# Seven products instead of eight in nearly every second expert product of a Sinkhorn-attention and mixture kernel, with the first product running a little ahead

## The chip, the core and the metric

The kernel runs on one core of a Trainium2 chip. The metric is the device time of one execution in microseconds (us). Engines are named as in the profile: PE (TensorE matmuls), PEld (TensorE weight loads), DVE (VectorE), ACT (ScalarE), POOL (GpSimd), SP (SyncE, which only issues transfers here).

## The reference, cut to what matters

```python
def _attn_ref(q, k, v, sort_net):            # 4 batches, 8 heads, 768 rows, 64 columns
    P = sort_net                             # 8x8 per head
    for _ in range(5):
        ...                                  # exp, then rows and columns divided by their sums
    k_sorted, v_sorted = ...                 # blocks of 96 rows mixed by P
    ...                                      # softmax attention inside each block
def _moe_ref(x, w_gate, w1, w2):             # x: 3072x512; w1: 8x512x1024; w2: 8x1024x512
    P = np.exp(x @ w_gate - max)
    for _ in range(8):
        ...                                  # P balanced over rows and columns
    for e in range(8):
        h = np.maximum(x @ w1[e], 0.0)
        out += P[:, e:e + 1] * (h @ w2[e])
```

Attention makes x; a balanced gate makes P; then each of eight experts does two matrix products with a relu between them, and its result is added to the output, weighted per row.

## The kernel before, in words

The first part does the attention and, woven into it, expert 0. It ends at about 134 us of the span. The stretch from there to about 173 us finishes expert 0, balances the gate (`balance`, eight rounds of short DVE operations with a small matmul in each) and starts expert 1. The rest, to the end, is experts 1 to 7.

For those experts a *product* is one pair (e, p): expert e on 1024 of the 3072 rows, so there are 21. Both matrix products of a pair can be done as a 2x2 block product by seven smaller products instead of eight, with sums of blocks made beforehand (Winograd's form of Strassen's scheme). The names of that scheme are s1 to s4 for sums of the left blocks, t1 to t4 (or x1 to x4) for sums of the right blocks, and u, v, w, x for accumulators in PSUM.

- `hidden(e, p, i, hT)` is a quarter of the first product with the relu. It is a generator of seven steps, here h0 to h6, each with two matmuls of 512 columns (L482). ACT copies three accumulators out (p1 L502, u2 L510, p5 L515), DVE makes c11, c22 and c12 from PSUM and a copy (L506, L518, L521: an addition with a floor at 0), and ACT makes c21 from the last accumulator u by a relu (L524). The four blocks go to the tile hT, which has two buffers.
- `output(e, p, i, hT)` is a quarter of the second product in the plain way: two results of 128 rows, eight matmuls of 512 columns each (L542), and for each one `gather`.
- `output7(e, p, i, hT)` is the same quarter by seven products: seven steps, here k0 to k6, each with four matmuls of 256 columns (L573). It has two accumulators, u (256 columns) and x (512 columns). u is taken out by DVE and goes on accumulating, so each later step on u waits for the gather before it. There are five gathers of 256 columns and one of 512. The pool of accumulators `oacc` has three buffers, so the x of a quarter gets the buffer that the u of the quarter before gives back.
- `gather` (L529) is one DVE operation: osbl += gate * PSUM.
- `sum_h(i, hT)` (L559) makes s1 to s4 for one quarter on POOL, four operations of 128x512. `sum_w` and `sum_w2` make the sums of the weights on POOL, eight operations each for an expert; they are taken one at a time from a queue by `sums(n)`.
- `scale0` (L602) multiplies expert 0's output by its gate on ACT; `sum_x` (L434) makes the sums of x on DVE.

In the loop `for n in range(1, 3 * (E - 1))` the quarter i of product n (`hidden`) is interleaved, step by step, with the quarter i of the second product of the pair before. The second product uses `output` for i = 0, for the whole of the first pair and for the whole of the last pair, and `output7` for the rest: 27 quarters in the plain way, 57 by seven products. After the loop the last pair's second product runs alone, in the plain way.

The order of each engine's queue is made by a scheduler when the program is built, from the order in which the code issues the operations; operations marked `pin` keep their order. Each engine works through its own queue in that order. A scheduler's rule seen in the built queues is that two engines do not read the same PSUM tile at once: the second waits for the first.

Of the kernel before, what the change touches and what calls it, by code (L numbers as in the profile page):

```python
# [25 lines left out]
def kernel(  # L26
# [55 lines left out]
    def load_w1(e):  # L82
        w1t[e] = wp.tile([128, 4, F], BF16, name="w1e")
        pin(nc.gpsimd.dma_start(out=w1t[e],
                                in_=moe_w1[e].rearrange("(kk k) f -> k kk f", k=128)))
# [37 lines left out]
        nc.vector.reciprocal(out=cs, in_=cs)  # L123
        nc.vector.tensor_mul(Pt, Pt, mkap(cs, [cs.ap[0], cs.ap[1], [0, 8]]))

    Prep = pp.tile([32, 8, 8, 16], BF16)
    for eng, i0 in ((nc.vector.tensor_copy, 0), (nc.scalar.copy, 4)):
        eng(Prep[:, i0:i0 + 4], mkap(P, [P.ap[0], [8, 4], [1, 8], [0, 16]], off=i0 * 8))

    xtT = xtp.tile([128, 4, N], BF16)  # L130
    osbl = xtp.tile([128, NT, Dm], F32)
    glog = xtp.tile([128, NT, E], F32)
    Pb = pp.tile([128, 32, 8], F32)
    Rt = {}

    def build_r(bb, eng, n):
# [230 lines left out]
    with ExitStack() as c2:  # L367
# [4 lines left out]
        for bb in range(1, B):  # L372
# [22 lines left out]
            for _ in ex:  # L395
# [5 lines left out]
        tc.tile_pool(name=name, bufs=bufs, reuse_waits="tile"))  # L401
    mpc, xcp, wq, wcq = late("mpc", 1), late("xcp", 1), late("wq", 2), late("wcq", 1)
    htp, fsp, hsp, w2q = late("htp", 2), late("fsp", 1), late("hsp", 3), late("w2q", 1)
    bk = ctx.enter_context(tc.tile_pool(name="bk", bufs=5, space=bass.MemoryType.PSUM,
                                        reuse_waits="tile"))
    op = ctx.enter_context(tc.tile_pool(name="op", bufs=3, space=bass.MemoryType.PSUM,
# [8 lines left out]
    def sum_w2(e):  # L415
        w2s[e] = (wcp.tile([128, 4, 4, Dm // 2], BF16, name="w2e") if e % 2 else
                  w2q.tile([128, 4, 4, Dm // 2], BF16, name="w2s"))
        for k in (0, 2):
            b11, b12 = (w2t[e][:, k:k + 2, d:d + 256] for d in (0, 256))
            b21, b22 = (w2t[e][:, 4 + k:6 + k, d:d + 256] for d in (0, 256))  # L420
            t1, t2, t3, t4 = (w2s[e][:, j, k:k + 2, :] for j in range(4))
            for a, b, c in ((b12, b11, t1), (b22, t1, t2), (b22, b12, t3), (b21, t2, t4)):
                pin(nc.gpsimd.tensor_tensor(out=c, in0=a, in1=b, op=ALU.subtract))
                yield
# [46 lines left out]
            yield  # L471

    TOP = 3.0e38

    def hidden(e, p, i, hT):
        ta, tb = (slice(1024 * p + 512 * j, 1024 * p + 512 * j + 512) for j in range(2))
        fs = slice(128 * i, 128 * i + 128)
        xs = slice(512 * p, 512 * p + 512)

        def add(ps, wa, xa, first):  # L480
            for kk in range(2):
                nc.tensor.matmul(ps, wa[:, kk, :], xa[:, kk, :],  # L482
                                 start=(first and kk == 0), stop=(kk == 1),
                                 skip_group_check=True)

        def wide(name):
            return fsp.tile([128, 512], F32, name=name)

        w1 = w1t[e]
        s1, s2, s4 = (wct[e][:, j, :, fs] for j in range(3))  # L490
        x1, x2, x4 = (xc[:, j, :, xs] for j in range(3))
        s3, x3 = w1[:, 0:2, 512 + 128 * i:640 + 128 * i], xtT[:, 0:2, tb]
        a11, a12 = w1[:, 0:2, fs], w1[:, 2:4, fs]
        a22 = w1[:, 2:4, 512 + 128 * i:640 + 128 * i]
        b11, b21, b22 = xtT[:, 0:2, ta], xtT[:, 2:4, ta], xtT[:, 2:4, tb]
        c11, c12 = hT[:, i, 0:512], hT[:, i, 512:1024]
# [12 lines left out]
        u2 = wide("u2")  # L509
        nc.scalar.copy(u2, u)  # L510
        yield
        v = bank()
        add(v, s1, x1, True)
        p5 = wide("p5")
        nc.scalar.copy(p5, v)  # L515
        yield
        add(u, s3, x3, False)
        nc.vector._custom_dve(TENSOR_ADD_SAT, out=c22, in0=u, in1=p5, s0=TOP, s1=0.0)  # L518
        yield
        add(v, s4, b22, False)  # L520
        nc.vector._custom_dve(TENSOR_ADD_SAT, out=c12, in0=v, in1=u2, s0=TOP, s1=0.0)  # L521
        yield
        add(u, a22, x4, False)
        nc.scalar.activation(out=c21, in_=u, func=AF.Relu)  # L524
        yield

    def gather(e, t, c, ps):
# [20 lines left out]
            yield  # L548


    hs = {}

    def sum_h(i, hT):
        s = hs[i] = hsp.tile([128, 4, 4, 128], BF16, name="hs")
        a11, a21, a12, a22 = (hT[:, f:f + 4, t + 128 * i:t + 128 * i + 128]
                              for f in (0, 4) for t in (0, 512))
        for a, b, o, c in ((a21, a22, ALU.add, 0), (s[:, 0], a11, ALU.subtract, 1),
                           (a11, a21, ALU.subtract, 2), (a12, s[:, 1], ALU.subtract, 3)):
            nc.gpsimd.tensor_tensor(out=s[:, c], in0=a, in1=b, op=o)  # L559

    def output7(e, p, i, hT):
        a, b = 8 * p + i, 8 * p + 4 + i
        ha, hb = slice(128 * i, 128 * i + 128), slice(512 + 128 * i, 640 + 128 * i)
        s1, s2, s3, s4 = (hs[i][:, j] for j in range(4))
        t1, t2, t3, t4 = (w2s[e][:, j] for j in range(4))
        u = op.tile([128, Dm], F32, name="oacc")[:, 0:256]
        x = op.tile([128, Dm], F32, name="oacc")
        x0, x1 = x[:, 0:256], x[:, 256:512]
        b11, b21, b22 = w2t[e][:, 0:4, 0:256], w2t[e][:, 4:8, 0:256], w2t[e][:, 4:8, 256:512]

        def add(ps, h, w, first):
            for fb in range(4):
                nc.tensor.matmul(ps, h[:, fb, :], w[:, fb, :], start=(first and fb == 0),  # L573
                                 stop=(fb == 3), skip_group_check=True)

        add(u, hT[:, 0:4, ha], b11, True)
        gather(e, a, 0, u)
        yield

        add(x0, hT[:, 4:8, ha], b21, True)  # L580
        yield
        add(u, s2, t2, False)
        gather(e, a, 256, u)
        yield
        add(x1, s1, t1, False)
        gather(e, b, 256, x1)
        yield
        add(u, s3, t3, False)
        gather(e, b, 256, u)
        yield  # L590
        add(x1, s4, b22, False)
        gather(e, a, 0, x)
        store(e, a)
        yield
        add(u, hT[:, 4:8, hb], t4, False)
        gather(e, b, 0, u)
        store(e, b)
        yield

    def scale0(ts):  # L600
        for t in ts:
            nc.scalar.activation(out=osbl[:, t, :], in_=osbl[:, t, :], func=AF.Copy,  # L602
                                 scale=glog[:, t, 0:1])

    def take(works):
        while works:
            works = [w for w in works if next(w, 0) is None]
# [18 lines left out]
            next(xs, 0)  # L626
    take([chain, xs])
    xs = sum_x(2)
    last = (1, 0, hT)
    queue = [sum_w2(1)]  # L630

    def sums(n):
        while n and queue:
            if next(queue[0], 0) is None:
                n -= 1
            else:
                queue.pop(0)

    for n in range(1, 3 * (E - 1)):
        e, p = 1 + n // 3, n % 3  # L640
        if n == 1 or p == 0 and e + 1 < E:
            load_w1(e + 1)
            queue.append(sum_w(e + 1))
        hT = htp.tile([128, 8, 1024], BF16, name="hT")
        for i in range(4):
            if last[0] == 1:
                scale0([8 * last[1] + i, 8 * last[1] + 4 + i])
            if n > 1 and i < 3:
                sum_h(i + 1, last[2])
            next(xs, 0)  # L650
            sums(3 if n == 1 or i == 3 else 1)
            take([hidden(e, p, i, hT),
                  (output7 if n > 1 and i else output)(*last[0:2], i, last[2])])
        if n == 1 or p == 0 and e + 1 < E:
            load_w2(e + 1)
            queue.append(sum_w2(e + 1))
        last = (e, p, hT)
    for i in range(4):
        take([output(*last[0:2], i, last[2])])


# [28 lines left out]
```

## Time and profile before

| | |
|---|---|
| time, median of 3 runs | 690.42 us (690.34 to 690.60) |
| the profiled execution's own time | 690.48 us |
| its span | 688.7 us |
| granted TensorE clock | 0.993 |
| PE busy | 666.7 us (97%) |
| DVE busy | 474.5 us (69%) |
| POOL busy | 432.4 us (63%) |
| ACT busy | 298.0 us (43%) |

The span runs from the first to the last instruction. The profiled execution took 1.8 us more than its span, and that lies around the span. Matmuls are pipelined, so "PE busy" says that PE had work in flight and not how fast it went; the time from the start of one matmul to the start of the next says that.

### The profile page before, as it was taken

How to read it: one execution, taken by the hardware profiler on the slowest of the kernel's cores; microseconds unless marked ns; L12 is line 12 of the kernel's file. 1: busy time of each engine (PE TensorE's matmuls, PEld its weight loads, DVE VectorE, ACT ScalarE, POOL GpSimd, SP SyncE). 2: the span in 40 equal slices, each digit the busy share in tenths (PEclk: the TensorE clock that was granted, in tenths of full speed). 3: DMA queues.
4: the chain of work that ended last, by engine and by line, in shares of the span. 5: the costliest groups of instructions: out<-in, count | busy, mean ns of one | idle time of the engine just before them, and what ended most of it. 6: DMA issues, size and time to landing. Idle time of an engine off the chain costs nothing.

```text
span 688.7 us, 12265 instructions
## 1 busy us (share of the span) xinstructions
PE 666.7 (97%) x4784; PEld 404.4 (59%) x4784; DVE 474.5 (69%) x968; ACT 298.0 (43%) x550; POOL 432.4 (63%) x411
## 2 busy tenths in 40 slices
PE   2999999999999999999999999999999999999997
PEld 1757666644446556556656655655665665565563
DVE  6627555578757778667767776767776777676773
ACT  3747646345953333343333433333333433334330
POOL 4532324202737987978977987789795998637520
PEclk9899999999999999999999999999999999999999
DMA  9897833403210340030302140034003120001213
GB/s 146 164 218 120 140 77 63 62 1 62 30 32 1 62 61 1 1 63 9 54 0 35 28 62 1 1 62 61 1 1 62 25 38 0 1 1 63 91 65 151
DMA packets 31755, 36.51 MB, mean 53 GB/s; under 512 B 2000, under 2 KB 24016, under 8 KB 31696
## 3 DMA queue, kind: packets, MB, share of 16 engines
q0 software_dynamic: 26400, 27.82, 25.5%
q1 hardware_dynamic: 5296, 7.90, 3.4%
q8 instruction: 37, 0.61, 0.4%
q14 instruction: 22, 0.18, 0.1%
HBM read 52.45 MB, written 6.29 MB: 85 GB/s over the span
## 4 chain that ended last, share of the span: by engine, by line
PE 91%; DVE 5%; ACT 1%; DMA 1%; issue 1%; SPq 0%; DVEq 0%
PE bk L482 36%; PE oacc L573 25%; PE oacc L542 13%; PE bank L297 5%; PE bank L304 5%; PE bank L232 2%; PE bank L152 1%; PE bank L243 1%; PE bank L215 1%; PE bank L196 1%; DMA vsb<-vs 1%; DVE cs L464 0%; PE bk L297 0%; PE bk L466 0%; PE bank L183 0%
## 5 line engine op out<-in xcount | busy, mean ns | idle before, releaser
L529 DVE SCALAR_TENSOR_TENSOR osbl<-oacc,glog,osbl 128x256 f32<-128x256 f32 (+1 forms) x396 | 214.8, 554 | 122.4 <-PE oacc L542 61.3
L559 POOL TENSOR_TENSOR hs<-hT 128x512 bf16<-128x512 bf16 x114 | 130.0, 1154 | 63.0 <-DVE hT L521 62.8
L482 PE MATMUL bk<-xtT,w1e 128*128 128x512 bf16 x504 | 149.9, 379 | 0.2 <-ACT u L510 0.2
L573 PEld LDWEIGHTS <-hs 128*128 128x128 bf16 x912 | 89.2, 98 | 59.0
L542 PE MATMUL oacc<-w2e,hT 128*128 128x512 bf16 x432 | 119.8, 379 | 0.0
L524 ACT ACTIVATE hT<-bk 128x512 bf16<-128x512 f32 x84 | 50.1, 597 | 153.0 <-PE bk L482 152.9
L482 PE MATMUL bk<-xc,wc 128*128 128x512 bf16 x336 | 99.9, 379 | 0.0
L573 PEld LDWEIGHTS <-hT 128*128 128x128 bf16 x684 | 66.9, 98 | 44.2
L510 ACT COPY u<-bk 128x512 f32<-128x512 f32 x84 | 49.2, 586 | 92.9 <-PE bk L482 92.8
L573 PE MATMUL oacc<-w2e,hs 128*128 128x256 bf16 x588 | 88.2, 273 | 0.0
L573 PE MATMUL oacc<-w2e,hT 128*128 128x256 bf16 x576 | 86.4, 273 | 0.0
L482 PEld LDWEIGHTS <-w1e 128*128 128x128 bf16 x672 | 65.8, 98 | 30.5 <-issue 1.4
L542 PEld LDWEIGHTS <-hT 128*128 128x128 bf16 x432 | 42.3, 98 | 50.8
L506 DVE CUSTOM_DVE_ANT_0 hT<-bk,p 128x512 bf16<-128x512 f32 x84 | 58.0, 691 | 18.4 <-PE bk L482 14.8
L559 POOL TENSOR_TENSOR hs<-hT,hs 128x512 bf16<-128x512 bf16 x57 | 65.8, 1154 | 1.5
L559 POOL TENSOR_TENSOR hs<-hs,hT 128x512 bf16<-128x512 bf16 x57 | 65.7, 1152 | 0.0
L502 ACT COPY p<-bk 128x512 f32<-128x512 f32 x84 | 49.2, 586 | 31.3 <-PE bk L482 31.3
L482 PEld LDWEIGHTS <-wc 128*128 128x128 bf16 x504 | 49.3, 98 | 22.2
L518 DVE CUSTOM_DVE_ANT_0 hT<-bk,p 128x512 bf16<-128x512 f32 x84 | 57.8, 688 | 4.5 <-PE bk L482 1.4
L515 ACT COPY p<-bk 128x512 f32<-128x512 f32 x84 | 49.3, 586 | 25.4 <-PE bk L482 25.4
L521 DVE CUSTOM_DVE_ANT_0 hT<-bk,u 128x512 bf16<-128x512 f32 x84 | 57.3, 682 | 0.1
L482 PE MATMUL bk<-xc,w1e 128*128 128x512 bf16 x168 | 50.0, 379 | 0.0
(106 smaller groups left out, 777.6 us busy)
## 6 DMA issues: line engine op xcount, KB each, us to landing
w1e<-in_moe_w_dram POOLq DMA_DIRECT2D x8, 1024.0 KB, 8.2
w2e<-in_moe_w_dram POOLq DMA_DIRECT2D x8, 1024.0 KB, 8.9
out_dram<-osbl SPq DMA_DIRECT2D x24, 256.0 KB, 2.0
vt<-in_v_dram POOLq DMA_DIRECT2D x3, 768.0 KB, 10.6
vsb<-vs SPq DMA_DIRECT2D x16, 97.5 KB, 4.6
vsb<-vs POOLq DMA_DIRECT2D x16, 97.5 KB, 4.1
qt<-in_q_dram POOLq DMA_DIRECT2D x4, 384.0 KB, 12.8
kt<-in_k_dram POOLq DMA_DIRECT2D x4, 384.0 KB, 13.4
```

What stands on the lines that cost most here:

```text
L482: nc.tensor.matmul(ps, wa[:, kk, :], xa[:, kk, :], start=(first and kk == 0), stop=(kk == 1), skip_group_check=True)
L502: nc.scalar.copy(p1, u)
L506: nc.vector._custom_dve(TENSOR_ADD_SAT, out=c11, in0=w, in1=p1, s0=TOP, s1=0.0)
L510: nc.scalar.copy(u2, u)
L515: nc.scalar.copy(p5, v)
L518: nc.vector._custom_dve(TENSOR_ADD_SAT, out=c22, in0=u, in1=p5, s0=TOP, s1=0.0)
L521: nc.vector._custom_dve(TENSOR_ADD_SAT, out=c12, in0=v, in1=u2, s0=TOP, s1=0.0)
L524: nc.scalar.activation(out=c21, in_=u, func=AF.Relu)
L529: nc.vector.scalar_tensor_tensor(out=o, in0=ps, scalar=glog[:, t, e:e + 1], in1=o, op0=ALU.mult, op1=ALU.add)
L542: nc.tensor.matmul(oacc, hT[:, fb, tt * 128:(tt + 1) * 128], w2t[e][:, fb, :], start=(fb == 0), stop=(fb == 7))
L559: nc.gpsimd.tensor_tensor(out=s[:, c], in0=a, in1=b, op=o)
L573: nc.tensor.matmul(ps, h[:, fb, :], w[:, fb, :], start=(first and fb == 0), stop=(fb == 3), skip_group_check=True)
```

## The change: what it does

- Every second product but the very first quarter goes by seven products: 83 quarters by `output7` and one by `output`, where there were 57 and 27.
- The roles of the block rows of h are exchanged (and with them those of w2 in `sum_w2`), so that s3 is c21 - c22. In `hidden`, one new DVE operation per quarter makes it from PSUM right after the last step: h3 = max(u, 0) - c22, 128x512, into a new tile h3. POOL makes three sums per quarter instead of four.
- For the first quarter of a pair, POOL makes the three sums in two parts, 128x384 when three quarters of hT are there and 128x128 when the last is.
- The loop runs over the second products and takes one step of `hidden` after each step of the second product. Two steps of `hidden` are taken before the loop, and the first quarter in the plain way has eight steps, so `hidden` is three steps ahead from then on. At the end the last pair's second product still runs alone, now by seven products, and the last three steps of the pair before it as well.
- The eight operations of `sum_w2(1)` are issued before the loop. `sums` takes 1, 1, 2, 2 operations in the four quarters of a product.
- Two small tiles (Prep, Pb) move to a pool that is freed after the attention, and a pool for h3 with two buffers is added.

```diff
-            b11, b12 = (w2t[e][:, k:k + 2, d:d + 256] for d in (0, 256))
-            b21, b22 = (w2t[e][:, 4 + k:6 + k, d:d + 256] for d in (0, 256))
+            b11, b12 = (w2t[e][:, 4 + k:6 + k, d:d + 256] for d in (0, 256))
+            b21, b22 = (w2t[e][:, k:k + 2, d:d + 256] for d in (0, 256))
...
         add(u, a22, x4, False)
         nc.scalar.activation(out=c21, in_=u, func=AF.Relu)
+        if i == 0:
+            h3[e, p] = h3p.tile([128, 4, 512], BF16, name="h3")
+        nc.vector.scalar_tensor_tensor(out=h3[e, p][:, i, :], in0=u, scalar=0.0, in1=c22,
+                                       op0=ALU.max, op1=ALU.subtract)
         yield
...
-    def sum_h(i, hT):
-        s = hs[i] = hsp.tile([128, 4, 4, 128], BF16, name="hs")
-        a11, a21, a12, a22 = (hT[:, f:f + 4, t + 128 * i:t + 128 * i + 128]
-                              for f in (0, 4) for t in (0, 512))
-        for a, b, o, c in ((a21, a22, ALU.add, 0), (s[:, 0], a11, ALU.subtract, 1),
-                           (a11, a21, ALU.subtract, 2), (a12, s[:, 1], ALU.subtract, 3)):
-            nc.gpsimd.tensor_tensor(out=s[:, c], in0=a, in1=b, op=o)
+    def sum_h(i, hT, f0=0, f1=4):
+        if f0 == 0:
+            hs[i] = hsp.tile([128, 3, 4, 128], BF16, name="hs")
+        s1, s2, s4 = (hs[i][:, j, f0:f1] for j in range(3))
+        a11, a21, a12, a22 = (hT[:, f + f0:f + f1, t + 128 * i:t + 128 * i + 128]
+                              for f in (4, 0) for t in (0, 512))
+        for a, b, o, c in ((a21, a22, ALU.add, s1), (s1, a11, ALU.subtract, s2),
+                           (a12, s2, ALU.subtract, s4)):
+            nc.gpsimd.tensor_tensor(out=c, in0=a, in1=b, op=o)
...
+    sums(8)
+    hTs = {0: hT}
+    def hiddens():
+        for n in range(1, 3 * (E - 1)):
+            hTs[n] = htp.tile([128, 8, 1024], BF16, name="hT")
+            yield from units(1 + n // 3, n % 3, hTs[n])
+    ahead = hiddens()
+    for _ in range(2):
+        next(ahead)
+    for n in range(1, 3 * (E - 1) + 1):
+        e, p, hT = 1 + (n - 1) // 3, (n - 1) % 3, hTs[n - 1]
+        d = 2 + n // 3
+        fetch = n == 1 or n % 3 == 0 and d < E
+        if fetch:
+            load_w1(d)
+            queue.append(sum_w(d))
         for i in range(4):
-            if last[0] == 1:
-                scale0([8 * last[1] + i, 8 * last[1] + 4 + i])
-            if n > 1 and i < 3:
-                sum_h(i + 1, last[2])
+            if e == 1:
+                scale0([8 * p + i, 8 * p + 4 + i])
             next(xs, 0)
-            sums(3 if n == 1 or i == 3 else 1)
-            take([hidden(e, p, i, hT),
-                  (output7 if n > 1 and i else output)(*last[0:2], i, last[2])])
...
-    for i in range(4):
-        take([output(*last[0:2], i, last[2])])
+            if i == 0 and n > 1:
+                sum_h(0, hT, 3)
+            if i < 3:
+                sum_h(i + 1, hT)
+            elif n < 3 * (E - 1):
+                sum_h(0, hTs[n], 0, 3)
+            sums(1 + i // 2)
+            for _ in (output7 if i or n > 1 else output)(e, p, i, hT):
+                next(ahead, 0)
+        if fetch:
+            load_w2(d)
+            queue.append(sum_w2(d))
```

In `output7` the indices of the block rows of hT and w2 are exchanged in the same way, and s3 is read from h3.

More of the change, by code (lines that the diff above doesn't have):

```diff
@@ L124 @@
         nc.vector.tensor_mul(Pt, Pt, mkap(cs, [cs.ap[0], cs.ap[1], [0, 8]]))
-    Prep = pp.tile([32, 8, 8, 16], BF16)
+    Prep = perp.tile([32, 8, 8, 16], BF16)
     for eng, i0 in ((nc.vector.tensor_copy, 0), (nc.scalar.copy, 4)):
@@ L132 @@
     glog = xtp.tile([128, NT, E], F32)
-    Pb = pp.tile([128, 32, 8], F32)
+    Pb = perp.tile([128, 32, 8], F32)
     Rt = {}
@@ L403 @@
     htp, fsp, hsp, w2q = late("htp", 2), late("fsp", 1), late("hsp", 3), late("w2q", 1)
+    h3p = late("h3p", 2)
     bk = ctx.enter_context(tc.tile_pool(name="bk", bufs=5, space=bass.MemoryType.PSUM,
@@ L473 @@
     TOP = 3.0e38
+    h3 = {}
     def hidden(e, p, i, hT):
@@ L563, in output7 @@
         ha, hb = slice(128 * i, 128 * i + 128), slice(512 + 128 * i, 640 + 128 * i)
-        s1, s2, s3, s4 = (hs[i][:, j] for j in range(4))
+        s1, s2, s4 = (hs[i][:, j] for j in range(3))
+        s3 = h3[e, p][:, :, ha]
         t1, t2, t3, t4 = (w2s[e][:, j] for j in range(4))
@@ L568, in output7 @@
         x0, x1 = x[:, 0:256], x[:, 256:512]
-        b11, b21, b22 = w2t[e][:, 0:4, 0:256], w2t[e][:, 4:8, 0:256], w2t[e][:, 4:8, 256:512]
+        b11, b21, b22 = w2t[e][:, 4:8, 0:256], w2t[e][:, 0:4, 0:256], w2t[e][:, 0:4, 256:512]
         def add(ps, h, w, first):
@@ L574, in add @@
                                  stop=(fb == 3), skip_group_check=True)
-        add(u, hT[:, 0:4, ha], b11, True)
+        add(u, hT[:, 4:8, ha], b11, True)
         gather(e, a, 0, u)
         yield
-        add(x0, hT[:, 4:8, ha], b21, True)
+        add(x0, hT[:, 0:4, ha], b21, True)
         yield
@@ L594, in output7 @@
         yield
-        add(u, hT[:, 4:8, hb], t4, False)
+        add(u, hT[:, 0:4, hb], t4, False)
         gather(e, b, 0, u)
@@ L628 @@
     xs = sum_x(2)
-    last = (1, 0, hT)
     queue = [sum_w2(1)]
@@ L637, in sums @@
                 queue.pop(0)
[L639 to L644, printed above, removed]
+    sums(8)
[14 more added lines that the diff above has]
+            queue.append(sum_w(d))
         for i in range(4):
-            if last[0] == 1:
-                scale0([8 * last[1] + i, 8 * last[1] + 4 + i])
-            if n > 1 and i < 3:
-                sum_h(i + 1, last[2])
+            if e == 1:
+                scale0([8 * p + i, 8 * p + 4 + i])
             next(xs, 0)
-            sums(3 if n == 1 or i == 3 else 1)
-            take([hidden(e, p, i, hT),
-                  (output7 if n > 1 and i else output)(*last[0:2], i, last[2])])
[L654 to L657, printed above, removed]
-    for i in range(4):
-        take([output(*last[0:2], i, last[2])])
+            if i == 0 and n > 1:
[10 more added lines that the diff above has]
+            queue.append(sum_w2(d))
 _INS = ['q', 'k', 'v', 'sort_net', 'moe_w_gate', 'moe_w1', 'moe_w2']
```

## The prediction

> **What bounds the kernel now.** I read the page's busy times first, then the busy times by stretch, the chain of waits, and the timeline of one quarter.
>
> ```profile
> 375.00:400.00 25.00, 25.00 (x159) 15.37 (x157) 18.13 (x33) 9.42 (x16) 21.68 (x21) 1.00 0.27 44
> 170.00:200.00 30.00, 29.76 (x137) 13.18 (x136) 20.53 (x31) 25.02 (x45) 14.76 (x14) 1.00 0.24 36
> 147.00:170.00 23.00, 21.35 (x109) 10.08 (x108) 19.38 (x56) 11.91 (x23) 1.60 (x2) 1.00 0.27 46
> ```
>
> The columns are PE, PEld, DVE, ACT and POOL busy, then the granted clock. In steady work (375 to 400) PE never stops, at clock 1.00, while DVE has 6.9 us and POOL 3.3 us free of 25. From 147 to 200 it is tighter: DVE is busy 19.4 of 23 us, then ACT 25.0 of 30.
>
> ```profile
> 379.34 0.86 PE oacc L542 x4
> 404.05 0.86 PE oacc L542 x4
> ...
> 670.25 13.83 PE oacc L542 x64
> 684.10 0.75 DVE osbl L529
> ```
>
> The chain of waits goes through the same plain matmuls every 404.05 - 379.34 = 24.71 us: that is one product. It ends in 64 plain matmuls in a row, 13.83 / 64 = 0.216 us each, and one gather.
>
> ```profile
> 481.05 0.60 PE L573 MATMUL oacc<-w2e,hs 128*128 128x256 bf16 x4
> 481.49 0.59 PE L482 MATMUL bk<-xc,wc 128*128 128x512 bf16 x2
> 481.92 0.60 PE L573 MATMUL oacc<-w2e,hs 128*128 128x256 bf16 x4
> 482.35 0.59 PE L482 MATMUL bk<-xtT,w1e 128*128 128x512 bf16 x2
> 482.79 0.60 PE L573 MATMUL oacc<-w2e,hs 128*128 128x256 bf16 x4
> ```
>
> Start to start, two matmuls of 512 columns take as long as four of 256: 0.434 us. I call this a block. A quarter is 14 blocks, 6.07 us.
>
> **The gain.** A plain quarter is 16 x 0.216 = 3.46 us of PE, one by seven products 7 x 0.434 = 3.04: 0.42 less. 83 - 57 = 26 quarters change: 26 x 0.42 = 11.0 us, all on PE and so on the path. Four of them are the tail, three lie in the first product, 19 in steady work.
>
> By one rule this gain would be a loss. The Trainium skill, in "TensorE: Matmul & The Clock Gate" (the part on sustained throughput), has the spacing of matmuls set by the weight load as well, with about 81 ns at 128 columns and 131 ns at 512; an estimate between them for 256 columns, about 98 ns, makes 28 small matmuls dearer than 16 large ones. The rows above disagree: 0.108 us is half of 0.216, so the loads are hidden.
>
> **Steady work: does VectorE keep up?** PE is relieved only if the others stay hidden.
>
> ```profile
> 481.69 0.48 DVE L529 SCALAR_TENSOR_TENSOR osbl<-oacc,glog,osbl 128x256 f32<-128x256 f32 x1 [0.51 <-PE oacc L573]
> 482.56 0.48 DVE L529 SCALAR_TENSOR_TENSOR osbl<-oacc,glog,osbl 128x256 f32<-128x256 f32 x1 [0.39 <-PE oacc L573]
> 483.09 0.69 DVE L518 CUSTOM_DVE_ANT_0 hT<-bk,p 128x512 bf16<-128x512 f32 x1
> 483.70 0.47 DVE L529 SCALAR_TENSOR_TENSOR osbl<-oacc,glog,osbl 128x256 f32<-128x256 f32 x1
> 484.09 0.68 DVE L521 CUSTOM_DVE_ANT_0 hT<-bk,u 128x512 bf16<-128x512 f32 x1
> 484.69 1.13 DVE L529 SCALAR_TENSOR_TENSOR osbl<-oacc,glog,osbl 128x512 f32<-128x512 f32 x2
> ```
>
> Back to back, operations overlap a little: a new one starts 0.39 us after a gather of 256 (483.70 to 484.09) and 0.60 to 0.61 after a custom addition. A gather starts 0.20 us after the last matmul of its block has been issued (block end 481.49, gather 481.69), a custom addition 0.30 after (482.79 to 483.09).
>
> ```profile
> 178.03 0.75 DVE L529 SCALAR_TENSOR_TENSOR osbl<-oacc,glog,osbl 128x512 f32<-128x512 f32 x1 [0.55 <-PE oacc L542]
> 178.70 0.68 DVE L518 CUSTOM_DVE_ANT_0 hT<-bk,p 128x512 bf16<-128x512 f32 x1
> 404.95 1.35 DVE L529 SCALAR_TENSOR_TENSOR osbl<-oacc,glog,osbl 128x512 f32<-128x512 f32 x2 [1.03 <-PE oacc L542]
> 141.85 0.39 PE L466 MATMUL bk<-cs,onesc 128*128 128x8 f32 x2 [0.27 <-DVE cs L464]
> 141.30 0.50 DVE L464 TENSOR_REDUCE cs<-glog 128x8 f32<-128x192 f32 x1
> ```
>
> After a gather of 512 the next starts after 0.67 us, or 0.60 if it is a gather too (1.35 - 0.75). A waiting PE starts 0.05 after DVE ends. The new h3 is not in this trace. Its nearest rows are the custom addition (0.69) and the 512 gather (0.75), with the same PSUM operand; I take the gather's 0.60 to the next start, with 0.55 and 0.70 as ends.
>
> A quarter then asks DVE for 3 x 0.60 + 0.60 (h3) + 5 x 0.39 + 0.65 = 5.0 us of 6.07. It fits on average; the order decides. The built queue runs, per quarter: gather k0, c22, gather k2, c12, gather k3, gather k4, h3, gather k5 (512), c11, gather k6. It has h3 wait for ACT's relu, since both read u:
>
> ```profile
> 669.22 0.59 PE L482 MATMUL bk<-xc,w1e 128*128 128x512 bf16 x2
> 669.85 0.60 ACT L524 ACTIVATE hT<-bk 128x512 bf16<-128x512 f32 x1 [1.96 <-PE bk L482]
> ```
>
> The relu starts 0.20 us after its block is issued and takes 0.60. From a quarter's start: h6 ends at 8 blocks, 3.47, the relu at 4.27. k4 ends at 3.90; its gather starts at 4.10, h3 at 4.49, gather k5 at 5.09, c11 at 5.76, gather k6 at 6.36, done at 6.84. The next x takes the buffer that this gather frees: it can start at 6.89 and is due at 16 blocks, 6.94. So the ordinary quarter closes with 0.05 to spare and costs nothing. At the start of a new hT, c11 also waits for k6, the last reader of the old hT: k6 ends at 5.64, c11 starts at 5.94, gather k6 at 6.54, x at 7.07: 0.13 late. That comes with each of 19 hT: 19 x 0.13 = +2.5 us, between 0 and 5.
>
> POOL's sums have slack. A product asks for nine operations of 512, three pairs of 384 and 128, and 16/3 weight sums:
>
> ```profile
> L559 POOL TENSOR_TENSOR hs<-hT,hs 128x512 bf16<-128x512 bf16 x57 | 65.8, 1154 | 1.5
> ```
>
> At 1.15 us that is about 20 us of 24.3. The small part of the split sums is due 4.3 us after the last relu's matmuls (three steps ahead plus two), and relu, three small sums and one large one between take about 3. The moved DMA issues of w1 and w2 stand beside these sums in POOL's queue, and the slack takes them.
>
> **The start.** Here h3 goes into the gate's chain.
>
> ```profile
> 162.87 0.20 DVE L469 RECIPROCAL cs<-cs 128x8 f32<-128x8 f32 x1
> 163.11 0.36 DVE L470 TENSOR_TENSOR glog<-glog,cs 128x192 f32<-128x192 f32 x1
> 163.09 0.60 ACT L524 ACTIVATE hT<-bk 128x512 bf16<-128x512 f32 x1 [1.21 <-PE bk L482]
> ```
>
> In the built queue the second h3 stands between these two DVE operations and waits for this relu, which ends at 163.69: the chain resumes about 164.4 and not 163.1, 1.3 us late, and the next matmul of the gate stands in PE's queue behind it. The first h3 mostly fills a wait. I count +1.4.
>
> ```profile
> 150.26 0.68 DVE L434 TENSOR_TENSOR xc<-xtT 128x1024 bf16<-128x1024 bf16 x1
> 175.27 1.60 DVE L434 TENSOR_TENSOR xc<-xtT 128x1024 bf16<-128x1024 bf16 x1
> 169.16 9.85 POOL L423 TENSOR_TENSOR w2e<-w2e 128x512 bf16<-128x512 bf16 x8 [6.75 <-PE oacc L304]
> ```
>
> The same `sum_x` operation takes 0.68 us while POOL is idle and 1.60 while it works. The Trainium skill, "GPSIMD Engine Reference", section 1, says that GpSimd shares SBUF ports with VectorE and contends with VectorE operations that have two SBUF inputs: these rows agree, and h3, with one PSUM input, would be spared by that rule, as the gathers are. In the first product POOL now works throughout, and two such operations stand just before a gather k0 on which k2 waits: 0.75 us each, +1.5. Then ACT, busy 25.0 of 30 us with `scale0`, makes relus late, h3 waits for them and gathers wait for h3: +1.2, between 0 and 3. POOL's first sums come after `sum_w2(1)`, which ends near 180 us; I make them due near 184, about when they are done: 0, at most 2. Start: +4.1, between 1.4 and 7.
>
> **The tail.** Without `hidden` between, only one block lies between two steps on u, while a gather needs 0.20 + 0.48 + 0.05 = 0.73: 0.30 is missing, three times in each of four quarters, 3.6 us. The built order puts halves of the next quarter's first block there, which saves some, but x waits once 0.95 us for a buffer, behind the last h3 and a 512 gather. Followed step by step, with the delays above, the 31 blocks end 2.9 us late (1.5 to 4). The last gather is 256 wide and not 512: 0.75 - 0.48 = -0.3.
>
> **Sum.** 690.48 (the profiled execution) - 11.0 + 2.5 + 4.1 + 2.9 - 0.3 = 688.7. The runs' median is 0.06 lower: 688.6 us.
>
> **The rivals.**
> *The covers hold.* No wait at a new hT, and a start that costs only the h3 in the chain, 1.4. The 25% of free DVE time in steady work speaks for it, the queues' order against. 690.4 - 11.0 + 1.4 + 2.9 - 0.3 = 683.4. Chance 0.25.
> *VectorE's chain from k4 to the next x becomes the bound.* It has 0.05 us to spare in 61 ordinary quarters and none in 19. If h3 or a start after a wait costs 0.12 more than I took, each ordinary quarter loses 0.07 and each of the 19 another 0.12: 4.3 + 2.3, so 695.2. It decides against the change from about 0.06 us more per quarter. h3's duration, seen only through neighbours, speaks for it. Chance 0.23.
> *POOL is late.* If small sums queue behind weight sums and a DMA issue, 1 us at each of six weight loads: 694.6. POOL's 4 free us per product speak against. Chance 0.05.
> *Small matmuls cost more than half of large ones.* If the 12 more weight loads per quarter showed at half a block for every four, 0.22 x 7 - 0.42 = +1.1 per quarter, 26 x 1.1 + 690.4 = 719. The timeline rows speak against it; this is the skill's rule above. Chance 0.02.
>
> **The numbers.** The forecast has 0.45. About 0.2% (1.4 us) is what a measurement of this kernel can tell from no change. The forecast lies 1.8 us below, with 2.5 either way: of its 0.45, 0.25 is faster by more than that, 0.16 within, 0.04 slower. With the first rival faster 0.50; within 0.16; slower 0.04 + 0.23 + 0.05 + 0.02 = 0.34. The range 682.5 to 695.5 takes in the forecast's own spread and the first two rivals.
>
> **What would show it.** In the profile after: a product every 24.3 us if ordinary quarters close, with PE waiting for DVE only at x of each first quarter (0.13); more than that means the second rival, and the place is x waiting for the gather k6. h3 near 0.7 us. PE waits near 164 us on the gate's chain. A tail of about 16.3 us after the last matmul on xc. Loads shown between small matmuls, or POOL ending PE's waits, would make it wrong.

## The result and the profile after

| | before | after |
|---|---|---|
| time, median | 690.49 us (20 runs, 689.67 to 691.87) | 687.88 us (20 runs, 686.51 to 690.72) |
| the profiled execution, its span | 690.48, 688.7 us | 687.08, 685.3 us |
| DVE, POOL busy | 474.5, 432.4 us | 545.9, 469.7 us |

The ratio is 0.9966, with a 95% interval of 0.9956 to 0.9977: the change is faster by 0.3%. The forecast was 688.6 us, in 682.5 to 695.5. The profiled execution ran 0.8 us below the median, and the times spread over 4.2 us where those of before spread over 2.2.

The busy times of the same three stretches (span, PE, PEld, DVE, ACT, POOL busy, granted clock, share of DMA):

```profile
375.00:400.00 25.00, 25.00 (x174) 16.86 (x173) 21.37 (x41) 9.68 (x17) 22.26 (x24) 1.00 0.23 41
170.00:200.00 30.00, 26.34 (x152) 14.56 (x151) 27.77 (x43) 24.88 (x44) 28.79 (x27) 1.00 0.20 36
147.00:170.00 23.00, 21.55 (x109) 10.21 (x108) 19.88 (x56) 11.85 (x23) 0.70 (x1) 1.00 0.00 0
```

In steady work PE is still busy all the time, with DVE 3.2 us more busy than before and POOL nearly as before. From 170 to 200 PE now lacks 3.7 us of 30: there DVE and POOL are both almost always busy. The new operation has one group of its own, near the 0.69 us of its neighbour row:

```profile
L530 DVE SCALAR_TENSOR_TENSOR h<-bk,hT 128x512 bf16<-128x512 f32 x84 | 57.2, 681 | 1.3 <-ACT hT L526 1.3
```

The timeline where one hT ends and the next begins (c11 is L508 now, gather L536, output7's matmuls L585, hidden's L484):

```profile
472.35 0.69 DVE L508 CUSTOM_DVE_ANT_0 hT<-bk,p 128x512 bf16<-128x512 f32 x1
...
496.66 0.69 DVE L508 CUSTOM_DVE_ANT_0 hT<-bk,p 128x512 bf16<-128x512 f32 x1
497.27 0.87 DVE L536 SCALAR_TENSOR_TENSOR osbl<-oacc,glog,osbl 128x256 f32<-128x256 f32 x2
...
497.19 0.59 PE L484 MATMUL bk<-xc,wc 128*128 128x512 bf16 x2
497.63 0.60 PE L585 MATMUL oacc<-w2e,hT 128*128 128x256 bf16 x4
```

From c11 to the same c11 one product later are 496.66 - 472.35 = 24.31 us, 0.40 less than the 24.71 of before. The two gathers in the third row are k6 of the old quarter and k0 of the new. The last PE row is the new x. It starts one block (0.44) after the row before it, so it waited for nothing, though k6's gather runs until about 497.27 + 0.48 = 497.75.

The start, with VectorE's, TensorE's and GpSimd's rows below one another:

```profile
163.72 0.69 DVE L530 SCALAR_TENSOR_TENSOR h<-bk,hT 128x512 bf16<-128x512 f32 x1 [0.43 <-ACT hT L526]
164.33 0.35 DVE L471 TENSOR_TENSOR glog<-glog,cs 128x192 f32<-128x192 f32 x1
...
183.39 3.70 DVE L435 TENSOR_TENSOR xc<-xtT,xc 128x1024 bf16<-128x1024 bf16 x1
187.01 0.47 DVE L536 SCALAR_TENSOR_TENSOR osbl<-oacc,glog,osbl 128x256 f32<-128x256 f32 x1
...
187.54 0.60 PE L585 MATMUL oacc<-w2e,hs 128*128 128x256 bf16 x4 [3.03 <-DVE osbl L536]
...
179.00 0.79 POOL L84 DMA_DIRECT2D w1e<-in_moe_w_dram  x1
179.81 3.40 POOL L570 TENSOR_TENSOR hs<-hT 128x512 bf16<-128x512 bf16 x3
183.17 2.26 POOL L570 TENSOR_TENSOR hs<-hs,hT 128x512 bf16<-128x512 bf16 x2
185.40 1.14 POOL L570 TENSOR_TENSOR hs<-hT,hs 128x512 bf16<-128x512 bf16 x1
187.13 1.15 POOL L330 TENSOR_TENSOR wc<-w1e 128x512 bf16<-128x512 bf16 x1 [0.59 <-DMA w1e<-in_moe_w_dram]
```

The second h3 stands in the gate's chain, as forecast. The large loss is another one: one `sum_x` operation (L435), 0.68 us when undisturbed, takes 3.70. It ends at 187.09, 0.55 us after GpSimd's run of sums ends (185.40 + 1.14 = 186.54). Behind it in VectorE's queue stands gather k0 of the first quarter by seven products, and PE waits 3.03 us for that gather.

In the tail, the two longest waits after the last matmul on xc are these:

```profile
666.88 0.60 PE L585 MATMUL oacc<-w2e,hT 128*128 128x256 bf16 x4 [0.44 <-DVE osbl L536]
...
669.93 0.81 PE L585 MATMUL oacc<-w2e,hT 128*128 128x256 bf16 x6 [0.19 <-DVE osbl L536]
```

Start to start, with the blocks between taken off, they cost 0.65 and 0.35 us; all of the tail's gaps add up to 2.7.

### The profile page after: what moved, and what is told of

It is laid out like the page before. It is cut to its first block, busy times and chain, and to the rows that moved or that the text cites. A ratio compares the mean times of both kernels' runs of the same rounds, so it can differ in the third digit from the quotient of the medians.

```text
span 685.3 us, 13204 instructions
## 1 busy us (share of the span) xinstructions
PE 658.8 (96%) x5096; PEld 435.2 (64%) x5096; DVE 545.9 (80%) x1156; ACT 297.8 (43%) x550; POOL 469.7 (69%) x492
## 4 chain that ended last, share of the span: by engine, by line
PE 69%; DVE 3%; issue 1%; DVEq 0%
PE oacc L585 35%; PE bk L484 34%; DVE osbl L536 2%; DVE xc L435 0%; DVE hT L508 0%; DVE h L530 0%; DVE hT L520 0%; DVE hT L523 0%; DVE xtT L435 0%; DVEq L536 0%; DVEq L520 0%
## 5 line engine op out<-in xcount | busy, mean ns | idle before, releaser
L536 DVE SCALAR_TENSOR_TENSOR osbl<-oacc,glog,osbl 128x256 f32<-128x256 f32 (+1 forms) x500 | 253.7, 522 | 11.2 <-PE oacc L585 2.5
L484 PE MATMUL bk<-xtT,w1e 128*128 128x512 bf16 x504 | 149.4, 379 | 0.0
L570 POOL TENSOR_TENSOR hs<-hT 128x512 bf16<-128x512 bf16 (+2 forms) x103 | 98.6, 967 | 60.0 <-DVE hT L523 59.7
L585 PEld LDWEIGHTS <-hs 128*128 128x128 bf16 x996 | 97.4, 98 | 65.7 <-issue 4.2
L585 PEld LDWEIGHTS <-hT 128*128 128x128 bf16 x996 | 97.4, 98 | 63.6 <-issue 1.9
L585 PE MATMUL oacc<-w2e,hT 128*128 128x256 bf16 x852 | 127.9, 273 | 1.1 <-DVE osbl L536 0.8
L585 PE MATMUL oacc<-w2e,hs 128*128 128x256 bf16 x708 | 105.5, 272 | 3.5 <-DVE osbl L536 3.5
L570 POOL TENSOR_TENSOR hs<-hT,hs 128x512 bf16<-128x512 bf16 (+2 forms) x103 | 98.7, 965 | 4.8
L570 POOL TENSOR_TENSOR hs<-hs,hT 128x512 bf16<-128x512 bf16 (+2 forms) x103 | 98.7, 965 | 4.5
L484 PE MATMUL bk<-xc,wc 128*128 128x512 bf16 x336 | 99.8, 379 | 0.0
L484 PEld LDWEIGHTS <-w1e 128*128 128x128 bf16 x672 | 65.8, 98 | 11.3 <-issue 0.2
L424 POOL TENSOR_TENSOR w2e<-w2e 128x512 bf16<-128x512 bf16 x32 | 37.1, 1174 | 44.2 <-PE oacc L304 43.8
L508 DVE CUSTOM_DVE_ANT_0 hT<-bk,p 128x512 bf16<-128x512 f32 x84 | 57.4, 684 | 1.4 <-issue 0.5
L530 DVE SCALAR_TENSOR_TENSOR h<-bk,hT 128x512 bf16<-128x512 f32 x84 | 57.2, 681 | 1.3 <-ACT hT L526 1.3
L484 PEld LDWEIGHTS <-wc 128*128 128x128 bf16 x504 | 49.3, 98 | 8.9 <-issue 0.2
L484 PE MATMUL bk<-xc,w1e 128*128 128x512 bf16 x168 | 50.3, 379 | 0.6 <-DVE hT L520 0.6
```

What stands on the lines that cost most here:

```text
L484: nc.tensor.matmul(ps, wa[:, kk, :], xa[:, kk, :], start=(first and kk == 0), stop=(kk == 1), skip_group_check=True)
L530: nc.vector.scalar_tensor_tensor(out=h3[e, p][:, i, :], in0=u, scalar=0.0, in1=c22, op0=ALU.max, op1=ALU.subtract)
L536: nc.vector.scalar_tensor_tensor(out=o, in0=ps, scalar=glog[:, t, e:e + 1], in1=o, op0=ALU.mult, op1=ALU.add)
```

## The experiments

Each kernel is the change with one edit; the times of before beside them are 690.3 to 690.7. Two theories are followed. By the first (the prediction's chain), what is lost sits at VectorE in every product. By the second (Theory A in the expectations of e2 and e3) it sits in one place of the start, where `sum_x` and GpSimd meet.

**The last pair in the plain way (e1).**

```diff
...
-            for _ in (output7 if i or n > 1 else output)(e, p, i, hT):
+            for _ in (output7 if (i or n > 1) and n < 3 * (E - 1) else output)(e, p, i, hT):
```

> The last pair's second product goes back to the plain way; all else is the changed kernel. By the tail term of the prediction (31 blocks, 2.9 us late; the trace of the changed kernel shows gaps of 2.7 us between its matmuls there) the plain tail asks for 4 x 0.42 = 1.7 us more of PE and loses the waits, so the whole is about 1 us shorter: 687 us. The rival is that the waits of the tail are hidden anyway by the last transfers: then the plain tail is 1.7 us longer, 689.6 us.

Measured: 686.67 us, ratio 0.9945 [0.9931, 0.9960]. The tail's gaps are gone. So seven products gain nothing in the tail: four quarters save 4 x 0.395 = 1.6 us of PE and cost 2.7 of waits. The start is as in the change: a sum_x of 3.68 us, and PE waits 3.01. The intervals of the two ratios, this one and the change's, overlap, so the gain rests on the gaps in the trace more than on the 1.2 us between the medians.

**sum_x of the last third of the rows earlier (e2).** The four operations are issued right behind those of the second third, in the stretch up to 177 us.

```diff
-    xs = sum_x(1)
+    def both():
+        yield from sum_x(1)
+        yield from sum_x(2)
+    xs = both()
...
-    xs = sum_x(2)
```

> The four sum_x operations of the third part of x are issued on VectorE right after those of the second part, while GpSimd is idle, and no longer between the gathers of the first product. Theory A (the 3.70 us sum_x operation beside GpSimd's sums holds the gather on which PE waits 3.03 us): each takes 0.68, the wait of 3.03 and that of 0.46 go, up to 4 x 0.6 us come into the gate's chain: 684.5 to 687 us. Theory B (the first product waits for GpSimd's first sums or for ScalarE whatever VectorE does): the wait stays near 3 us under another name, and the added work makes it 688 to 690 us.

Measured: 685.47 us (685.02 to 686.22), ratio 0.9925 [0.9913, 0.9938]. The instructions of sum_x, in the line's own view (duration in ns: min, median, max):

```profile
L435 DVE TENSOR_TENSOR xc<-xtT,xc x6: 683/688/1640, 136.7 to 176.2; 128x1024 bf16<-128x1024 bf16 x6
```

The longest takes 1.64 us, and the 3.03 us wait is gone. The median is 2.4 us lower than the change's. The traces place about 1.5 us of it in the start, where PE's gaps between 141.8 and 206 us add up to 1.5 less than the change's: a wait of 0.64 for the gate and some of 0.27 to 0.42 take the rest of the 3.0 back. The times spread over 1.2 us and not 4.2; what makes the change's slower runs slow is not shown.

**The same four operations early, but on GpSimd (e3).**

```diff
-            pin(nc.vector.tensor_tensor(out=c, in0=a, in1=b, op=ALU.subtract))
+            pin((nc.gpsimd if p == 2 else nc.vector).tensor_tensor(
+                out=c, in0=a, in1=b, op=ALU.subtract))
...
```

> The same four operations as early, but on GpSimd, which is idle from 136 to 169 us. Theory A: VectorE has none of them in the first product and none in the gate's chain; GpSimd needs about 4 x 2.2 us; 684 to 685 us, unless GpSimd's work stretches the gate's own operations with two SBUF inputs (192 elements, 0.36 us each), which would cost up to 2 us. Theory B: 688 us or more.

Measured: 686.38 us, ratio 0.9938 [0.9926, 0.9950]. GpSimd's two later operations, VectorE's step of the gate beside them, and PE behind it:

```profile
163.39 2.13 POOL L435 TENSOR_TENSOR xtT<-xtT 128x1024 bf16<-128x1024 bf16 x1 [23.78 <-PE bk L297]
165.47 2.13 POOL L435 TENSOR_TENSOR xc<-xtT,xc 128x1024 bf16<-128x1024 bf16 x1
...
166.40 1.42 DVE L472 TENSOR_TENSOR glog<-glog,cs 128x192 f32<-128x192 f32 x1
...
170.21 0.39 PE L468 MATMUL bk<-cs,onesc 128*128 128x8 f32 x2 [1.41 <-DVE cs L466]
```

The gate's product with two SBUF inputs takes 1.42 us (0.36 beside an idle GpSimd) and ends at 167.82, 0.22 us after GpSimd's operation (167.60). This time the gate pays, and PE waits 1.41. The contention moved with the operations. No load runs here (the share of the DMA engines from 163 to 168 us is 0.00), and VectorE is held up for one GpSimd operation only.

**h3 twice (e4).** The h3 instruction is issued two times.

> The h3 operation is issued twice, with the same output: 0.60 us more of VectorE in each of 84 quarters. By the prediction's chain (the next x waits for the gather k6, no time to spare) PE would lose about 0.6 us in each quarter, some 45 us: 733 us. If x instead takes the buffer of the x before, which is free 1 us earlier, the quarter has about 0.9 us of VectorE free and closes nearly as before: 688 to 691 us, with a later start and tail by 0.6 to 2 us.

Measured: 693.11 us, ratio 1.0040 [1.0025, 1.0054], above the second case's range and far below the first. The rows of c11 one product apart, and those of one new x with gathers k6 and k0 beside it:

```profile
496.52 0.68 DVE L508 CUSTOM_DVE_ANT_0 hT<-bk,p 128x512 bf16<-128x512 f32 x1
...
520.91 0.68 DVE L508 CUSTOM_DVE_ANT_0 hT<-bk,p 128x512 bf16<-128x512 f32 x1
...
497.02 0.60 PE L587 MATMUL oacc<-w2e,hT 128*128 128x256 bf16 x4
497.12 0.86 DVE L538 SCALAR_TENSOR_TENSOR osbl<-oacc,glog,osbl 128x256 f32<-128x256 f32 x2
```

With 0.6 us more of VectorE in each quarter a product takes 24.39 us and not 24.31, 0.02 more per quarter. So VectorE has nearly 0.6 us to spare in each quarter, not 0.05. And the new x (497.02) starts before gather k6 does (497.12). Of the 6.0 us between the two profiled executions, 2.0 are gaps of PE in steady work (206 to 660 us) and 4.2 lie in the start again, where the shifted queues put a sum_x beside the whole run of GpSimd's sums:

```profile
177.99 7.07 DVE L435 TENSOR_TENSOR xc<-xtT 128x1024 bf16<-128x1024 bf16 x1
...
183.37 1.14 POOL L572 TENSOR_TENSOR hs<-hT,hs 128x512 bf16<-128x512 bf16 x1
...
186.31 1.01 PE L484 MATMUL bk<-xc,w1e 128*128 128x512 bf16 x2 [5.82 <-DVE hT L520]
```

It ends at 185.06, again 0.55 us after GpSimd's sums (183.37 + 1.14 = 184.51).

**A copy in place of the subtraction (e8).** In the last third of the rows `sum_x` copies its first operand; what it subtracts is left out.

```diff
-            pin(nc.vector.tensor_tensor(out=c, in0=a, in1=b, op=ALU.subtract))
+            if p == 2:
+                pin(nc.vector.tensor_copy(out=c, in_=a))
+            else:
+                pin(nc.vector.tensor_tensor(out=c, in0=a, in1=b, op=ALU.subtract))
```

> The four sum_x operations of the third part of the rows stay where the change has them but copy their first operand, so they have one SBUF input and not two; what they subtract is left out. If the 3.70 us are the price of a second SBUF input while GpSimd works, no such operation takes over 0.7 us, the 3.03 us wait for the gather is gone and the time is 685 to 686 us. If any VectorE operation between two SBUF tiles is held up while GpSimd works, one of the four again takes over 1.5 us, PE waits some 1 to 3 us at the first gathers and the time is 687 to 689.

Measured: 686.85 us, ratio 0.9959 [0.9940, 0.9977], and the second theory's picture:

```profile
183.12 3.15 DVE L436 COPY xc<-xtT 128x1024 bf16<-128x1024 bf16 x1
```

One input is held up like two. The Trainium skill, "SBUF — State Buffer", section "Who interferes with whom", has both: VectorE and GpSimd share one pair of ports under an exclusive lock, and it counts copies in a two-port mode among the operations that take it, beside those with two SBUF inputs. The row agrees with that, if the copy ran in such a mode, which the profile does not tell. The lock is described there as held for one instruction; these holds last through three to six GpSimd instructions, so something more is at work here.

**The transfer moved away (e9), and the sums taken away (e10).** While GpSimd makes those sums, expert 2's first weights (1 MB) are also being loaded. These two runs part the causes. In e9 the load and the sums of its weights are issued two quarters later:

```diff
-        if fetch:
+        if fetch and n > 1:
...
         for i in range(4):
+            if fetch and n == 1 and i == 2:
+                load_w1(d)
+                queue.append(sum_w(d))
```

> In the change the stretched sum_x ends near 187.1, when two things come together: GpSimd goes idle (186.54) and the transfer of expert 2's first weights lands (187.13). Here that load, and the eight sums that follow it, are issued two quarters later, while GpSimd's sums of h stay in place. If GpSimd's back-to-back sums hold the VectorE operation up, a sum_x near 183 again takes over 2.5 us, ends some 0.55 us after GpSimd next goes idle, PE waits 2 to 4 us for the gather, and the time is 687 to 690 us. If the transfer into SBUF holds it up, all sum_x take under 1.7 us, PE's wait is gone and the time is 685 to 686.

In e10 the first pair's second product goes in the plain way, without sums of h:

```diff
...
-            for _ in (output7 if i or n > 1 else output)(e, p, i, hT):
+            for _ in (output7 if n > 1 else output)(e, p, i, hT):
```

> The whole second product of the first pair goes in the plain way, so GpSimd makes no sums of h before the second product, while expert 2's first weights are loaded where the change loads them. If GpSimd's sums hold sum_x up, every sum_x takes under 1.7 us though the transfer runs beside it; the 3 us wait is gone, three quarters lose their gain (3 x 0.395 = 1.2) and the time is 685 to 686.7 us. If the transfer holds it up, a sum_x again takes over 2 us until the weights land, and the time is 687 to 690.

Measured: e9 686.38 us, ratio 0.9935 [0.9916, 0.9954]; e10 693.69 us, ratio 1.0048 [1.0032, 1.0063]. The same stretch, 182 to 184 us, in the change, then in e9 with the sum_x of its timeline, then in e10 with its own (POOL busy is the fifth of the busy times; behind the clock stand the share of the DMA engines and GB/s):

```profile
182.00:184.00 2.00, 2.00 (x15) 1.32 (x14) 1.87 (x3) 2.00 (x5) 2.00 (x3) 1.00 1.11 211
```

```profile
182.00:184.00 2.00, 1.99 (x15) 1.26 (x14) 1.75 (x4) 2.00 (x5) 2.00 (x2) 1.00 0.00 0
```

```profile
182.68 0.68 DVE L435 TENSOR_TENSOR xc<-xtT,xc 128x1024 bf16<-128x1024 bf16 x1
```

```profile
182.00:184.00 2.00, 2.00 (x11) 0.88 (x9) 1.77 (x3) 2.00 (x5) 0.00 (x0) 1.00 1.10 207
```

```profile
183.09 0.68 DVE L435 TENSOR_TENSOR xc<-xtT,xc 128x1024 bf16<-128x1024 bf16 x1
```

With GpSimd's sums and the transfer together the operation takes 3.70 us; with the sums alone 0.68, with the transfer alone 0.68. Neither rival as written is right: it takes both. Without a transfer, VectorE gets in between two GpSimd instructions. This is seen best in e12 (below), where the transfer has landed by then:

```profile
191.24 1.66 DVE L435 TENSOR_TENSOR xc<-xtT,xc 128x1024 bf16<-128x1024 bf16 x1
...
191.21 1.15 POOL L570 TENSOR_TENSOR hs<-hT,hs 128x512 bf16<-128x512 bf16 x1
192.31 1.60 POOL L330 TENSOR_TENSOR w1e<-w1e 128x512 bf16<-128x512 bf16 x1
```

VectorE waits for one GpSimd instruction, and the next is 0.45 longer because it waits for VectorE. With the transfer running, VectorE waited until GpSimd had nothing to do, in the change and in six of the runs (e1, e4, e5, e6, e8, e12): 2.98 to 7.79 us. In all but one of these the transfer's last packet and the end of GpSimd's last sum lie within 0.4 us of each other, so it could be the end of the transfer that lets VectorE in. e6, the kernel with four sums on GpSimd further down, parts the two:

```profile
182.46 2.98 DVE L434 TENSOR_TENSOR xc<-xtT,xc 128x1024 bf16<-128x1024 bf16 x1
...
183.75 1.14 POOL L565 TENSOR_TENSOR hs<-hT,hs 128x512 bf16<-128x512 bf16 x1
186.59 1.16 POOL L330 TENSOR_TENSOR wc<-w1e 128x512 bf16<-128x512 bf16 x1 [1.70 <-DMA w1e<-in_moe_w_dram]
```

The sum_x ends at 185.44, 0.55 after GpSimd's sum (184.89), while GpSimd waits for the weights until 186.59. So there it is GpSimd's falling idle, and not the end of the transfer, that ends the hold. The section of the Trainium skill named above says that a DMA never contends with a compute engine; the one stall that it names is that of a DMA whose descriptors GpSimd makes, held up by VectorE. Here VectorE is the one held up, and a load that was issued from GpSimd's own queue decides whether it gets its turn, so the rule does not hold as it stands; why is open.

In e9 the time moved: the wait for the gather is gone, but the weight sums now stand in GpSimd's queue ahead of the small sums of the next product, and PE waits there for 2.15 us:

```profile
205.75 0.28 PE L585 MATMUL oacc<-w2e,hs 128*128 128x256 bf16 x1 [2.15 <-POOL hs L570]
```

The time expected for e10 was missed by 7 us. All of it comes from a side effect: the plain way has eight steps a quarter, so hidden is six steps ahead for the rest of the kernel and not three. The next two settle that.

**The same with the lead kept at three (e11), and the change with a lead of six (e12).** In e11 hidden's step is left out once in each of three quarters; in e12 five steps are taken before the loop.

```diff
-    for _ in range(2):
+    for _ in range(5):
         next(ahead)
```

> With the whole first second-product in the plain way and hidden six steps ahead, the time was 693.7 us, a product in steady work took 24.77 us and not 24.31, and no sum_x took over 1.14 us. Here three steps of hidden are held back, so that hidden is three steps ahead as in the change. If the lead alone made that product longer, it takes 24.31 us again, and without the 3 us wait at the first gathers the time is 685 to 686.7 us. If the plain first product brings the loss itself, the time stays at 692 to 694.

> The change with five steps of hidden taken before the loop and not two, so hidden is six steps ahead. If the lead sets how the two chains meet at VectorE and the accumulators, a product takes 24.77 us as it did with six steps before: 19 x 0.46 = 8.7 us more, 694 to 698 us. If a longer lead only gives GpSimd more time, a product stays at 24.31 us and the time is 686 to 689.

Measured: e11 684.97 us, ratio 0.9920 [0.9901, 0.9938]; e12 699.71 us, ratio 1.0135 [1.0119, 1.0152]. A row of e12's chain of waits comes back every product:

```profile
583.69 1.44 PE bk L484 x6
608.47 1.45 PE bk L484 x6
633.24 1.45 PE bk L484 x6
```

With a lead of six a product takes 24.77 us, in e10 and in e12; in e11 it takes 24.31 as in the change. 19 x 0.46 = 8.7 us, all of the loss of e10 (693.7 - 685.0 = 8.7). e12 has a sum_x of 7.17 us on top. The profile names no releaser for the 0.46, so its mechanism stays open. And e11 says what the three quarters by seven products in the first pair are worth where the change puts them: without them the median is 2.9 us lower (the profiled execution 2.0).

**Without a lead (e5).** The two steps before the loop are left out, so hidden is one step ahead.

> The two steps of hidden ahead of the loop are left out, so hidden is one step ahead in the loop and not three. The prediction counted the lead as part of what covers the split sums: the small ones are due two steps (1.7 us) sooner, about 2.6 us after the last relu's matmuls, while relu, three small sums and a large one between take about 3 to 3.5. By this PE waits 0.5 to 1 us for GpSimd at each of 18 boundaries between products: 697 to 706 us. Rival: the queue of GpSimd is empty enough at that place (it idles 0.95 to 2 us before the small sums), then PE waits at most 0.3 us each and the time is 687 to 692.

Measured: 699.00 us, ratio 1.0122 [1.0104, 1.0139]. PE's waits from 206 to 660 us (in total, times, longest), and the start:

```profile
PE oacc L585 <- POOL hs L570: 2.9, 9, 0.3
```

```profile
180.19 7.79 DVE L435 TENSOR_TENSOR xc<-xtT 128x1024 bf16<-128x1024 bf16 x1
```

The total lies in the range of the expectation's first case, but for another reason as well. The small sums make PE wait only 0.3 us each, as the rival said. The two profiled executions are 12.3 us apart (699.42 and 687.08). Start to start, PE's gaps are 5.2 us longer than the change's from 140 to 206 us, where it waits 6.89 us behind the sum_x of 7.79, and 4.8 us longer from 206 to 660 us; nearly all of these 4.8 lie at the nine waits for GpSimd, some 0.5 us each start to start. These are what the lead covers for GpSimd.

**Four sums on GpSimd, no h3 (e6).**

> GpSimd makes all four sums of a quarter again and VectorE's h3 is left out, with all 83 quarters by seven products. GpSimd is busy 372.8 of 454 us in steady work; 93 more sums of 0.96 us make 462 and it becomes the bound: at least 8 us plus waits at each product's start, 700 to 720 us, with PE waiting for hs. Rival: the sums are only shifted within GpSimd's free time and the time stays at 687 to 692.

Measured, one run: 716.0 us. Busy times and PE's waits from 206 to 660 us:

```profile
206.00:660.00 454.00, 435.17 (x2937) 289.68 (x2938) 335.51 (x629) 164.61 (x280) 439.26 (x457) 0.98 0.17 28
```

```profile
PE oacc L580 <- POOL hs L565: 19.9, 11, 3.9
```

GpSimd is busy 439 of 454 us and ends PE's waits. Seven products in nearly every quarter pay only because VectorE makes the third sum.

**The two gains together (e7).** sum_x early and the last pair in the plain way.

> Both gains at once: the sum_x of the third part of the rows is issued in the stretch where GpSimd is idle, and the last pair's second product goes in the plain way. If the 3.03 us wait at the first gather and the tail's short waits are two separate costs, the two gains add: the change's 687.9 less 2.4 (early sum_x) less 1.2 (plain tail) gives 684.3 us, 683.8 to 685. If the plain tail's gain was noise, 685.5 as with the early sum_x alone.

Measured: 684.74 us (684.09 to 685.24), ratio 0.9916 [0.9901, 0.9932]: 5.6 us faster than before, 3.1 faster than the change. The medians' gains nearly add: 2.4 and 1.2 alone, 3.1 together. e11 is as fast with the change's own tail; its edit and the plain tail were not run together.

## Why the prediction was right or wrong

The sign and the size are right. Of the terms, the gain and the tail were about right, one was not there, and the start was right only as a sum, by luck.

| step | forecast | measured |
|---|---|---|
| 26 quarters save PE time | -11.0 | 26 x 0.395 = -10.3 |
| 19 new hT: x late | +2.5 | 0 |
| start | +4.1 | +4.1 |
| tail | +2.9 | +2.7 |
| last gather | -0.3 | -0.05 |

The start's 4.1 is PE's idle time from 141.8 to 206 us, summed over all matmuls start to start less their own times, with the gate's small ones taken as nothing: 6.1 before, 10.2 after. The last gather's 0.05 is the time from the end of the last matmul's own 0.22 or 0.11 us to the end of the span: 4.81 before, 4.76 after. Small gaps elsewhere are 0.2. Together 690.48 - 10.3 + 4.1 + 2.7 - 0.05 + 0.2 = 687.1, against 687.08 of the profiled execution.

- **The gain.** Right, 0.025 us per quarter too high: a large matmul takes 0.2158 us and a small one 0.1092, from the two product times, so a quarter saves 0.395.
- **The weight loads.** The rival at 719 us falls, and with it, for this kernel, the rule of the Trainium skill's "TensorE: Matmul & The Clock Gate" that was weighed there: 0.1092 us per small matmul hold through all of steady work.
- **x at a new hT.** This step failed. It counted that the next x takes the buffer which gather k6 of u gives back, and the kernel's description says the same of the three buffers of `oacc`. The row at 497.63 shows x starting 0.12 us before that gather ends, so it had another buffer, free earlier; in e4 x starts even before that gather does. With it falls the rival of VectorE's chain (695.2): two h3 in each quarter (e4) cost steady work 0.02 us a quarter.
- **The start.** Right as a sum, wrong in its parts. The h3 in the gate's chain delays the gate by 1.2 us, but PE has other work there: its idle time up to 175 us is 5.8 us before and 5.9 after. So the 1.4 is 0.1. The two sum_x were priced at 0.75 each, from a row of 1.60 beside a working GpSimd; one of them took 3.70 and cost 3.0. The step that failed is this price: the row it came from had no transfer beside it. Late relus and the rest cost about 1.
- **The shared ports.** In steady work, beside a GpSimd that is busy 22.3 of 25 us, h3 and the gathers of 256 keep 0.68 and 0.48 us; what grew are operations between SBUF tiles. The rule cited from the Trainium skill's "GPSIMD Engine Reference", section 1, pointed to the right operations, and these rows agree; the size of the loss it doesn't tell.
- **The tail.** Right: 2.7 for 2.9. But the text did not set it against the tail's own gain of 1.6, which would have told the tail's change to be a loss.
- **GpSimd** has the slack that was counted: in the change no wait of PE in steady work ends with it, and without the lead it is 0.3 us late (e5).
- **The first rival** (683.4) had steady work right, and missed the contention.

## What to carry to other kernels

When work is moved to GpSimd, look for every VectorE operation between SBUF tiles that now runs beside it, and at what stands behind it in VectorE's queue: one such operation cost PE 3.0 us here, and the 84 further h3 of e4, which have an operand in PSUM, cost it 2.0 in steady work. Set the gain of each place against the waits of that same place; steady work won 19 x 0.395 = 7.5 us, and the first product and the tail, after their own gains of 1.2 and 1.6, lost 2.9 and 1.1 of it. And two chains woven by hand have a phase: three steps of lead cost nothing, six cost 0.46 us in every product.

## What the runs showed of the hardware

A VectorE operation between SBUF tiles, beside back-to-back GpSimd sums and a load that GpSimd's queue issued, did not end until GpSimd had fallen idle: 2.98 to 7.79 us for work of 0.68. Without that load no sum_x took over 1.72 us: its own time, and what was left of one GpSimd operation.

A wait can also cost clock. e4 after its wait of 5.82 us, which ended at 186.31 (the clock is the number ahead of the last two):

```profile
184.00:186.00 2.00, 0.00 (x0) 0.00 (x0) 2.00 (x3) 0.00 (x0) 1.26 (x2) 0.50 0.28 51
186.00:188.00 2.00, 1.69 (x5) 0.59 (x5) 2.00 (x4) 0.60 (x1) 2.00 (x3) 0.50 0.00 0
188.00:190.00 2.00, 2.00 (x7) 0.77 (x6) 0.82 (x3) 1.79 (x3) 1.92 (x3) 0.63 0.00 0
```

TensorE goes at half clock until about 189 us. After the change's wait of 3.03 us the clock stayed at 1.00, but after a wait of 2.00 us in e6, which ended at 495.61, it was 0.50 from 496 to 498 us. So the length of a wait alone does not tell; what does is not shown here.
